# Attention, a feed-forward block and a gated convolution block in fp32 products split three ways: the places of TensorE's operands in SBUF

## The chip, the cores and the metric

The kernel runs on one core of a Trainium2 chip. Its engines are TensorE (PE: matrix products, with the load of the stationary operand shown as PEld), VectorE (DVE), ScalarE (ACT), GpSimd (POOL) and SyncE (SP, which here issues the DMAs). The metric is the time of one execution on the device in microseconds; lower is better. Three executions of the kernel before took 1298.81, 1300.61 and 1300.77 us, a median of 1300.61 us.

## The reference

The batch is 8, the sequence 576 long, the model 512 wide, so there are 4608 tokens in 36 tiles of 128.

```python
# 1. attention in chunks of 64 tokens, 8 heads of 64
scores = scale * np.matmul(q_c, k_c.transpose(0, 1, 2, 4, 3))
attn = np.exp(scores - np.max(scores, axis=-1, keepdims=True))
attn = attn / (np.sum(attn, axis=-1, keepdims=True) + 1e-09)
x = np.matmul(attn, v_c)                    # put together as [B, S, 512]
# 2. feed-forward block, 512 -> 2048 -> 512, with a residual
xn = (x - mu) / np.sqrt(var + 1e-06) * g_ln
x = x + np.maximum(xn @ w_ch1, 0.0) @ w_ch2
# 3. gated block, 512 -> 1024 -> 512
h = np.maximum(x @ w_in, 0.0)
conv_out = sum(conv_w[k] * hp[:, k:k + S] for k in range(3))   # hp: h padded by one token
out = (h * (1.0 / (1.0 + np.exp(-conv_out)))) @ w_out
```

Inputs and output are fp32.

## The kernel before

Every large product is done in the type fp32r, in which TensorE streams fp32 words. An operand is split into a high part (a cast to fp32r) and a low part (the rest), and `mm3` (lines 113 to 116) adds three products into a PSUM bank: low stationary part times high streamed part (L114), high times low (L115), high times high (L116). Each of the three is one LDWEIGHTS of a stationary operand of 128 columns and one MATMUL that streams 256 or 512 columns.

There are four such products, and they follow each other:

- **up** (w_ch1): `product` (L588) for each of 9 slabs of 512 tokens. The weights `w` (tiles `w1`) are stationary, and the normalised tokens `xc`, seven combinations of 256-column blocks per slab, are streamed: 256 columns at a time, 12 matmuls in a row on one `xc`. The 36 tiles of attention (L385 to L475, plain fp32 products of 64 columns and transposes of 128) lie between them.
- **down** (w_ch2): `Down` (L688). `split` (L700) makes `hh` and `hl`, the high and low part of a tile of the up product that was stored in HBM and loaded again as `hr`. They are stationary, the weights `w2` (trace names `w` and `wd`) are streamed, 512 columns. 12 matmuls use one `hh`/`hl`.
- **gate** (w_in): `Gate` (L884). The weights are stationary, the tokens `xb` (`x_parts`, L805: four tiles of `[128, 2, 512]` for even slabs and four for odd ones) are streamed, 512 columns.
- **out** (w_out): `outtile` (L874). 128 columns of the rings `Gh` and `Gl` (L865, one pair for each of 8 blocks of 128 features, 1152 tokens long) are stationary, the weights `wo` (trace names `w` and `wx`) are streamed, 512 columns.

The order of the work is written out by hand: a list of steps at the head (`START`), then loops in the order in which they stand (`manual_schedule`). SBUF is given out by pools, some from the left end and some from the right end, tile after tile in the order of allocation. Two tiles named `fill` of 56 floats, 224 bytes per partition, are never read or written: one ends the pool `const` (L104), the other is alone in the pool `edge` at the right end (L524, L525). With them every tile that a fp32r matmul reads starts at a multiple of 256 bytes.

**Distance** here is the byte address of the streamed operand, minus the byte address of the stationary operand that is loaded while it streams (that of the next matmul), modulo 256 bytes. The addresses are those that the built program holds. In the kernel before it is 0 for all fp32r matmuls. Of the plain fp32 work, the products of `rk` and `rq` have distance 0, those of `rv` and `pt` distance 32, the transposes of `pp` distance 64 and those of `xn` distance 128.

Of the kernel before, what the change touches and what calls it, by code (L numbers as in the profile page):

```python
# [8 lines left out]
F32 = mybir.dt.float32  # L9
F32R = mybir.dt.float32r  # L10
# [34 lines left out]
def attn_moe_moe2(  # L45
# [63 lines left out]
    def split(hi, lo, src):  # L109
        nc.scalar.copy(hi, src)  # L110
        nc.vector.tensor_tensor(out=lo, in0=src, in1=hi.bitcast(F32), op=ALU.subtract)
# [366 lines left out]
    class Slab:  # L478
# [24 lines left out]
            return {1: b11, 5: getattr(self, "t1", None), 6: b11, 2: b21, 7: b12, 4: b21, 3: b22}[n]  # L503

        def u(self, n):
            t = self.xc[n] = xc_p.tile([128, 2, 2, 256], F32R, tag=f"xc{n}", name="xc")
            nc.scalar.copy(t[:, 0], self.of(n))

        def v(self, n):
# [11 lines left out]


    with tc.manual_schedule():
        edge = tc.alloc_tile_pool(name="edge", bufs=1, side="right", reuse_waits="tile")  # L524
        edge.tile([128, 56], F32, name="fill")  # L525
        wb_p = tc.alloc_tile_pool(name="wb", bufs=1, reuse_waits="tile")
        wa_p = tc.alloc_tile_pool(name="wa", bufs=1, reuse_waits="tile")
        xc_p = tc.alloc_tile_pool(name="xc", bufs=1, side="right", reuse_waits="tile")
        su_p = tc.alloc_tile_pool(name="su", bufs=1, side="right", reuse_waits="tile")
        at = Attention()  # L530
# [15 lines left out]
        def one(step):  # L546
            kind, i = step[0], int(step[1:])
            if kind in "atmng":
                getattr(blocks[i // 4], kind)(i % 4)
            elif kind == "W":  # L550
                blocks[i // 4].W(i % 4, nc.sync)
            elif kind == "w":
                blocks[i // 4].W(i % 4, nc.scalar)
            elif kind == "s":
                blocks[i // 4].s(i % 4)
            elif kind in "hl":
                getattr(blocks[i // 7], kind)(i % 7)
            elif kind in "juv":
                getattr(slabs[0], kind)(i)
            elif kind == "S":  # L560
                at.S(i, (4, 6, 0, 4, 0, 2)[i])
            elif kind == "V":
                at.V(i, (4, 6, 0, 4)[i])
            elif kind == "P":
                at.P(i, i % 2 * 2 if i > 3 else 2)
            elif kind == "L":
                at.L(i, late=i > 5)
            elif kind in "y":
                at.x(i)
            elif kind == "z":  # L570
                at.T(i)
            else:
                getattr(at, kind)(i)
# [109 lines left out]
        for tv in range(4, NTILE, 2):  # L683

            t = 28 * (tv // 4 - 1) + (13 if tv % 4 else 0)
            session({4: 7, 6: 14}.get(tv, t), tv)

        class Down:  # L688
# [10 lines left out]

            def split(self, f):  # L700
                t = self.hr[f % 8][:, f // 8 * 2:f // 8 * 2 + 2].rearrange("p a n -> p (a n)")
                self.hh = dp.tile([128, 512], F32R, tag="hh", bufs=2, name="hh")
                self.hl = dp.tile([128, 512], F32R, tag="hl", bufs=2, name="hl")
                nc.scalar.activation(out=self.hh, in_=t, func=AF.Relu)  # L704
                nc.vector.scalar_tensor_tensor(  # L705
                    out=self.hl, in0=t, scalar=0.0, in1=self.hh.bitcast(F32), op0=ALU.max,
                    op1=ALU.subtract,
                )
                return self.hh, self.hl
# [9 lines left out]
        dp = None  # L719
        for p in range(NS + 1):  # L720
            if p + 1 < NS:
                slabs[p + 1] = Slab(p + 1)
            for G in range(4):
                for s, (n, lag) in enumerate(SLOTS):
                    t = 28 * p + 7 * G + s
# [14 lines left out]
                    if p == NS - 1:  # L740
                        if (G, s) == (0, 5):
                            at.p.release()
                            dp = tc.alloc_tile_pool(name="dp", bufs=1, reuse_waits="tile")
# [51 lines left out]
        def split_x2(i, kk):  # L795
            t = x2r[i]
            split(
                xb[i % 2][0][kk // 2][:, kk % 2].rearrange("p (a t) -> p a t", t=32),
                xb[i % 2][1][kk // 2][:, kk % 2].rearrange("p (a t) -> p a t", t=32),
                t[:, :, kk, :],  # L800
            )
            if kk == KD - 1 and i + 1 < NS:
                load_x2(i + 1)

        def x_parts(pool, name):  # L805
            return [[pool.tile([128, 2, 512], F32R, name=f"{name}{2 * i + j}") for j in range(2)]
                    for i in range(2)]

        xb = [x_parts(pbx, "xb0")]
        todo = [(p, f) for p in range(NS) for f in F_ORDER]  # L810
        downs = {0: down}
        xrs = {}
        ended = None
        for n, (p, f) in enumerate(todo):
            hh, hl = parts
# [21 lines left out]
            if (p, f) == (0, 15):  # L837
# [4 lines left out]
                for i in range(16):  # L842
                    pool, tag = wb_tags[i]
# [17 lines left out]
        pb = tc.alloc_tile_pool(name="pb", bufs=1, reuse_waits="tile")  # L861
        RING = 1152
        Gh, Gl = {}, {}

        def ring(f):  # L865
            Gh[f] = pb.tile([128, RING], F32R, name=f"Gh{f}")
            Gl[f] = pb.tile([128, RING], F32R, name=f"Gl{f}")

        for f in (7, 6, 5):
            ring(f)  # L870
        for f in range(5):
            ring(f)
        xb.append(x_parts(pb, "xb1"))
        def outtile(T, tail=False):  # L874
            ps = bank[4 + T % 4] if tail else bank[2 + T % 2]
# [114 lines left out]
        pb.release()  # L990
        pbx.release()
        wb_p.release()
        edge.release()


# [41 lines left out]
```

## Time and profile before

| what | value |
|---|---|
| median of three executions | 1300.61 us |
| profiled execution | 1302.26 us, its span 1300.5 us |
| PE busy | 1251.4 us, 96% of the span |
| PEld busy | 1097.7 us, 84% |
| DVE busy | 744.6 us, 57% |
| ACT busy | 614.7 us, 47% |
| mean granted clock of TensorE | 0.976 |

Busy time is the time in which an engine has an instruction in it. On PE matmuls overlap, and the end that a row gives to a matmul is modelled: the pace is read from starts, not from durations. Idle time of an engine that is not the bottleneck costs nothing.

### The profile page before, as it was taken

To read this page: it belongs to the slowest core of one execution; us is meant where nothing else is said; L and a number is where in the kernel's file an instruction comes from. 1 tells how busy PE (TensorE), PEld (TensorE's weight loads), DVE (VectorE), ACT (ScalarE), POOL (GpSimd) and SP (SyncE) were. 2 spreads that over 40 slices of the span, in tenths; PEclk is the share of its full clock that TensorE was granted. 3 is DMA by queue.
4 is the path that set the end of the run, shared out by engine and by line. 5 is a ranking of instruction groups with operands and counts; after the bars stand their busy time and mean duration, and the time that the engine had idled before them with its cause. 6 is when DMAs were issued, how large, how long until landed. Compare 5 with 4: busy or idle time off the path is not lost.

```text
span 1300.5 us, 23238 instructions
## 1 busy us (share of the span) xinstructions
PE 1251.4 (96%) x9096; PEld 1097.7 (84%) x9096; DVE 744.6 (57%) x1430; ACT 614.7 (47%) x1510; POOL 78.6 (6%) x172
## 2 busy tenths in 40 slices
PE   5569999999999999999999999999999999999998
PEld 4469999999999998778888888888788888888887
DVE  7896456456456457577734333433886556655550
ACT  6775555555546345344322222222675555555541
POOL 0000000000000000000000000000121111111100
PEclk6689999999999999999999999999999999999999
DMA  9724644644545268486444355432111011101001
GB/s 266 212 98 154 205 164 160 205 157 166 202 155 185 108 219 291 135 305 217 154 161 162 122 177 185 161 120 87 41 57 57 26 56 58 57 25 57 25 25 49
DMA packets 127021, 177.70 MB, mean 137 GB/s; under 512 B 12736, under 2 KB 72128, under 8 KB 126912
## 3 DMA queue, kind: packets, MB, share of 16 engines
q1 hardware_dynamic: 126912, 176.22, 40.3%
q8 instruction: 71, 1.16, 0.4%
q14 instruction: 38, 0.31, 0.1%
HBM read 110.13 MB, written 66.06 MB: 135 GB/s over the span
## 4 chain that ended last, share of the span: by engine, by line
PE 86%; DVE 5%; DMA 4%; ACT 3%; SPq 1%; issue 1%; ACTq 0%; DVEq 0%
PE banks L114 27%; PE banks L115 27%; PE banks L116 27%; PE banks L385 3%; DMA rk<-in_k_dram 2%; PE banks L467 1%; DMA w<-in_moe_w_ch_dram 1%; PE banks L425 1%; DVE w L157 1%; DMA wd<-in_moe_w_ch_dram 1%; DVE hl L705 1%; DMA x2d<-x2T 0%; DVE w L152 0%; SPq L366 0%; DVE xr L160 0%
## 5 line engine op out<-in xcount | busy, mean ns | idle before, releaser
L114 PE MATMUL banks<-xc,w 128*128 128x256 f32 x1008 | 291.7, 289 | 9.6 <-DVE u L160 6.9
L115 PE MATMUL banks<-xc,w 128*128 128x256 f32 x1008 | 287.4, 285 | 0.0
L116 PE MATMUL banks<-xc,w 128*128 128x256 f32 x1008 | 287.2, 285 | 0.0
L704 ACT ACTIVATE hh<-hr 128x512 fp32r<-128x512 f32 x144 | 91.1, 632 | 257.4 <-PE banks L116 257.0
L705 DVE SCALAR_TENSOR_TENSOR hl<-hr,hh 128x512 fp32r<-128x512 f32 x144 | 99.3, 689 | 191.5 <-ACT hh L704 189.1
L114 PEld LDWEIGHTS banks<-xc,w 128*128 128x128 f32 x1008 | 195.8, 194 | 12.1 <-DVE u L160 7.5
L115 PEld LDWEIGHTS banks<-xc,w 128*128 128x128 f32 x1008 | 196.0, 194 | 0.0
L116 PEld LDWEIGHTS banks<-xc,w 128*128 128x128 f32 x1008 | 195.6, 194 | 0.0
L114 PE MATMUL banks<-w,hl 128*128 128x512 f32 x396 | 154.8, 391 | 0.0
L115 PE MATMUL banks<-w,hh 128*128 128x512 f32 x396 | 154.1, 389 | 0.0
L116 PE MATMUL banks<-w,hh 128*128 128x512 f32 x396 | 154.1, 389 | 0.0
L160 DVE TENSOR_TENSOR u<-banks,u 128x512 f32<-128x512 f32 x108 | 74.4, 689 | 123.1 <-ACT u L614 91.5
L920 DVE SCALAR_TENSOR_TENSOR cv<-hb,cw_sb,cv 128x510 f32<-128x510 f32 (+31 forms) x256 | 117.3, 513 | 0.6
L614 ACT COPY u<-banks 128x512 f32<-128x512 f32 x108 | 63.9, 592 | 111.0 <-PE banks L116 110.3
L114 PE MATMUL banks<-xb,w 128*128 128x512 f32 x288 | 112.7, 391 | 2.2 <-ACT hb L905 1.9
L115 PE MATMUL banks<-xb,w 128*128 128x512 f32 x288 | 112.1, 389 | 0.0
L116 PE MATMUL banks<-xb,w 128*128 128x512 f32 x288 | 112.1, 389 | 0.0
L411 ACT ACTIVATE pp<-banks,mx 128x64 f32<-128x64 f32 x288 | 86.8, 335 | 26.8 <-DVE x L439 20.4
L114 PEld LDWEIGHTS banks<-w,hl 128*128 128x128 f32 x396 | 74.3, 188 | 17.6 <-DVE hl L705 2.4
L116 PEld LDWEIGHTS banks<-w,hh 128*128 128x128 f32 x396 | 74.3, 188 | 15.4
L115 PEld LDWEIGHTS banks<-w,hh 128*128 128x128 f32 x396 | 74.3, 188 | 15.3
L907 POOL COPY hal<-hb 128x2 f32<-128x2 f32 x64 | 41.8, 652 | 727.3 <-ACT hb L905 727.3
(106 smaller groups left out, 2183.1 us busy)
## 6 DMA issues: line engine op xcount, KB each, us to landing
hd<-u SPq DMA_DIRECT2D x144, 256.0 KB, 3.2
hr<-hd SPq DMA_DIRECT2D x72, 512.0 KB, 3.6
w<-in_moe_w_ch_dram SPq DMA_DIRECT2D x27, 512.0 KB, 7.2
rv<-in_v_dram SPq DMA_DIRECT2D x36, 256.0 KB, 5.5
xd<-x SPq DMA_DIRECT2D x36, 256.0 KB, 2.2
xr<-xd SPq DMA_DIRECT2D x36, 256.0 KB, 4.5
x2d<-x2T SPq DMA_DIRECT2D x36, 256.0 KB, 2.0
x2r<-x2d SPq DMA_DIRECT2D x36, 256.0 KB, 3.8
```

Source lines behind the costliest of these rows:

```text
L114: nc.tensor.matmul(ps, ll, rh, start=first, stop=False, **kw)
L115: nc.tensor.matmul(ps, lh, rl, start=False, stop=False, **kw)
L116: nc.tensor.matmul(ps, lh, rh, start=False, stop=last, **kw)
L157: nc.vector.tensor_tensor(out=out, in0=a, in1=b, op=ALU.subtract)
L160: nc.vector.tensor_tensor(out=out, in0=a, in1=b, op=ALU.add)
L385: nc.tensor.matmul(ps[half(c), e, j, :], lt[half(e), j, c, :], rt[half(e), j, c, :], start=True, stop=True,)
L411: nc.scalar.activation(out=pp[:, j, e, :], in_=self.both[T][:, e, j, :], func=AF.Exp, scale=SCALE, bias=mx[:, e, j:j + 1], accum_out=sm[:, ...
L614: nc.scalar.copy(flat(t), bank[to])
L704: nc.scalar.activation(out=self.hh, in_=t, func=AF.Relu)
L705: nc.vector.scalar_tensor_tensor(out=self.hl, in0=t, scalar=0.0, in1=self.hh.bitcast(F32), op0=ALU.max, op1=ALU.subtract,)
L907: nc.gpsimd.tensor_copy(out=hal[:, f, :], in_=hb[:, 512:514])
L920: nc.vector.scalar_tensor_tensor(out=cv[:, a:e], in0=hb[:, a + tap:e + tap], scalar=cw_sb[:, tap, f:f + 1], in1=cv[:, a:e], op0=ALU.mult, ...
```

## The change

Four kinds of tiles get room behind them or a shift inside them, and the tile at the right end of SBUF goes. An `xc` tile is 1032 floats long and its first 1024 are used; the `xb` tiles likewise; a ring is 1160 long and its first 1152 are used. Thus tiles that follow each other start 32 bytes apart modulo 256. `hh` and `hl` are 544 long, and 512 of them are used from float `f % 8 * 4` on, 16 bytes further for each `f`; their two buffers start 128 bytes apart modulo 256.

```diff
--- before.py
+++ after.py
@@ -503,7 +503,8 @@
             return {1: b11, 5: getattr(self, "t1", None), 6: b11, 2: b21, 7: b12, 4: b21, 3: b22}[n]
 
         def u(self, n):
-            t = self.xc[n] = xc_p.tile([128, 2, 2, 256], F32R, tag=f"xc{n}", name="xc")
+            t = xc_p.tile([128, 1032], F32R, tag=f"xc{n}", name="xc")[:, :1024]
+            t = self.xc[n] = t.rearrange("p (h k n) -> p h k n", h=2, k=2)
             nc.scalar.copy(t[:, 0], self.of(n))
 
         def v(self, n):
@@ -521,8 +522,6 @@
 
 
     with tc.manual_schedule():
-        edge = tc.alloc_tile_pool(name="edge", bufs=1, side="right", reuse_waits="tile")
-        edge.tile([128, 56], F32, name="fill")
         wb_p = tc.alloc_tile_pool(name="wb", bufs=1, reuse_waits="tile")
         wa_p = tc.alloc_tile_pool(name="wa", bufs=1, reuse_waits="tile")
         xc_p = tc.alloc_tile_pool(name="xc", bufs=1, side="right", reuse_waits="tile")
@@ -699,8 +698,9 @@
 
             def split(self, f):
                 t = self.hr[f % 8][:, f // 8 * 2:f // 8 * 2 + 2].rearrange("p a n -> p (a n)")
-                self.hh = dp.tile([128, 512], F32R, tag="hh", bufs=2, name="hh")
-                self.hl = dp.tile([128, 512], F32R, tag="hl", bufs=2, name="hl")
+                at = slice(f % 8 * 4, f % 8 * 4 + 512)
+                self.hh = dp.tile([128, 544], F32R, tag="hh", bufs=2, name="hh")[:, at]
+                self.hl = dp.tile([128, 544], F32R, tag="hl", bufs=2, name="hl")[:, at]
                 nc.scalar.activation(out=self.hh, in_=t, func=AF.Relu)
                 nc.vector.scalar_tensor_tensor(
                     out=self.hl, in0=t, scalar=0.0, in1=self.hh.bitcast(F32), op0=ALU.max,
@@ -803,8 +803,11 @@
                 load_x2(i + 1)
 
         def x_parts(pool, name):
-            return [[pool.tile([128, 2, 512], F32R, name=f"{name}{2 * i + j}") for j in range(2)]
-                    for i in range(2)]
+            def one(at):
+                t = pool.tile([128, 1032], F32R, name=f"{name}{at}")[:, :1024]
+                return t.rearrange("p (k n) -> p k n", k=2)
+
+            return [[one(2 * i + j) for j in range(2)] for i in range(2)]
 
         xb = [x_parts(pbx, "xb0")]
         todo = [(p, f) for p in range(NS) for f in F_ORDER]
@@ -863,8 +866,8 @@
         Gh, Gl = {}, {}
 
         def ring(f):
-            Gh[f] = pb.tile([128, RING], F32R, name=f"Gh{f}")
-            Gl[f] = pb.tile([128, RING], F32R, name=f"Gl{f}")
+            for to, name in ((Gh, "Gh"), (Gl, "Gl")):
+                to[f] = pb.tile([128, RING + 8], F32R, name=f"{name}{f}")[:, :RING]
 
         for f in (7, 6, 5):
             ring(f)
@@ -990,7 +993,6 @@
         pb.release()
         pbx.release()
         wb_p.release()
-        edge.release()
 
 
 # ---- launch: one core; inputs and outputs as the reference has them ----
```

The instructions of the built program are the same as before on every engine, in the same order and with the same waits: 6784 on PE, 1422 on DVE, 1042 on ACT, 571 on SP, 134 on POOL. Shapes and the inner steps of the operands are the same too. Addresses are what differs. The distances of the fp32r matmuls that are followed by another fp32r matmul become:

| product | matmuls | distance 0 | distances | changes from one matmul to the next |
|---|---|---|---|---|
| up | 2989 | 422 | 0, 32, ... to 192, about 430 each | 252 |
| down | 1728 | 108 | all multiples of 16, 108 each | 145 |
| gate | 864 | 128 | 0, 32, ... to 192, 79 to 224 each | 720 |
| out | 863 | 78 | 0, 32, ... to 224, 36 to 144 each | 495 |
| all | 6444 | 736 | 5708 are not 0 | 1612 |

Of the other tiles, `x2r` (the loaded tokens of the gated block), the last two `wo` tiles and the output tiles `ob` start at 224, 224 and 160 modulo 256 where before they started at 0, 0 and 32.

## Rows read from the trace of the kernel before

**Rows 1.** The page: span, busy time of the engines, PE's slices, its granted clock.

```profile
span 1300.5 us, 23238 instructions
...
PE 1251.4 (96%) x9096; PEld 1097.7 (84%) x9096; DVE 744.6 (57%) x1430; ACT 614.7 (47%) x1510; POOL 78.6 (6%) x172
...
PE   5569999999999999999999999999999999999998
...
PEclk6689999999999999999999999999999999999999
```

**Rows 2.** The chain that ended last, by engine and line.

```profile
PE 86%; DVE 5%; DMA 4%; ACT 3%; SPq 1%; issue 1%; ACTq 0%; DVEq 0%
PE banks L114 27%; PE banks L115 27%; PE banks L116 27%; PE banks L385 3%; DMA rk<-in_k_dram 2%; PE banks L467 1%; DMA w<-in_moe_w_ch_dram 1%; PE banks L425 1%; DVE w L157 1%; DMA wd<-in_moe_w_ch_dram 1%; DVE hl L705 1%; DMA x2d<-x2T 0%; DVE w L152 0%; SPq L366 0%; DVE xr L160 0%
```

**Rows 3.** Groups of instructions: out<-in, count | busy, mean ns | idle before them.

```profile
L115 PE MATMUL banks<-xc,w 128*128 128x256 f32 x1008 | 287.4, 285 | 0.0
...
L115 PE MATMUL banks<-w,hh 128*128 128x512 f32 x396 | 154.1, 389 | 0.0
...
L115 PE MATMUL banks<-xb,w 128*128 128x512 f32 x288 | 112.1, 389 | 0.0
...
L115 PE MATMUL banks<-w,Gh 128*128 128x512 f32 x216 | 84.0, 389 | 0.0
...
L115 PE MATMUL banks<-wd,hh 128*128 128x512 f32 x180 | 70.1, 389 | 0.0
...
L115 PE MATMUL banks<-wx,Gh 128*128 128x512 f32 x72 | 28.0, 389 | 0.0
...
L385 PE MATMUL banks<-rk,rq 64*64 64x64 f32 x1152 | 25.7, 237 | 14.6 <-DMA rk<-in_k_dram 13.4 <-DVE mx L402 1.0
...
L385 PE MATMUL banks<-rv,pt 64*64 64x64 f32 x1152 | 24.4, 237 | 7.1 <-ACT pt L431 7.0
```

**Rows 4.** Timeline of PE, 207.5 to 220.5: start, duration (us), instruction (first and last of 107).

```profile
207.56 0.28 PE L115 MATMUL banks<-xc,w 128*128 128x256 f32 x1
...
220.28 0.28 PE L116 MATMUL banks<-xc,w 128*128 128x256 f32 x1
```

**Rows 5.** Timeline of PE, 690 to 713: first and last of 103 rows.

```profile
689.69 0.39 PE L115 MATMUL banks<-wd,hh 128*128 128x512 f32 x1
...
712.81 0.39 PE L115 MATMUL banks<-w,hh 128*128 128x512 f32 x1
```

**Rows 6.** Timeline of all engines, 527.2 to 530.3, around a wait of PE.

```profile
528.42 0.19 PEld L114 LDWEIGHTS banks<-w,hl 128*128 128x128 f32 x1 [0.37 <-DVE hl L705]
528.42 0.50 PE L114 MATMUL banks<-w,hl 128*128 128x512 f32 x1
528.53 0.19 PEld L115 LDWEIGHTS banks<-w,hh 128*128 128x128 f32 x1
...
528.76 0.40 PE L115 MATMUL banks<-w,hh 128*128 128x512 f32 x1
...
529.91 0.39 PE L114 MATMUL banks<-w,hl 128*128 128x512 f32 x1
```

**Rows 7.** Timeline of PE, 525.3 to 527.3, after another wait.

```profile
525.42 0.50 PE L114 MATMUL banks<-w,hl 128*128 128x512 f32 x1
525.76 0.40 PE L115 MATMUL banks<-w,hh 128*128 128x512 f32 x1
...
527.16 0.40 PE L115 MATMUL banks<-w,hh 128*128 128x512 f32 x1
```

**Rows 8.** Timeline of PE, 205.5 to 208.6: two transposes of attention.

```profile
205.70 1.04 PE L425 MATMUL banks<-ident,pp 128*128 128x128 f32 x8
206.57 1.04 PE L467 MATMUL banks<-ident,xn 128*128 128x128 f32 x8
```

**Rows 9.** DMA issues: out<-in, count, KB each, median us to landing.

```profile
x2r<-x2d SPq DMA_DIRECT2D x36, 256.0 KB, 3.8
```

## The prediction

> **What bounds the kernel now.** I read the page first. PE is busy for 1251.4 of 1300.5 us, from the fourth of its 40 slices on nearly without a hole, and from the same slice on the granted clock is at nine tenths or more; DVE and ACT have an instruction in them for 57% and 47% of the span [rows 1]. The chain of waits says the same: 86% of it is PE, and three lines, L114 to L116, have 27% each [rows 2]. These are the three products of `mm3`. So the end is set by the pace of the fp32r matmuls, and the next thing to know is that pace and how much of it is not streaming.
>
> The groups by line give the counts [rows 3]: each of the three lines has 1008 matmuls of 256 columns and 396 + 288 + 216 + 180 + 72 = 1152 of 512 columns, so there are 3024 short and 3456 long ones. The pace is read from starts in the timeline, since ends are modelled. Short: 106 steps from 207.56 to 220.28 us, 120.0 ns each [rows 4]. Long: 102 steps from 689.69 to 712.81 us, 226.7 ns each [rows 5]. 3024 x 120.0 + 3456 x 226.7 is 1146 us, 88% of the span: the whole kernel is these two numbers, and attention is most of the rest.
>
> The two paces differ by 106.7 ns for 256 columns, 0.417 ns a column, which is the 2.4 GHz level. Streaming alone is then 106.7 and 213.3 ns, and both paces are 13.3 ns above it. That remainder is the same for a short and a long matmul, so it does not go with the streamed columns; it goes with the change of matmul or with the load of 128 stationary columns, which is there once in each.
>
> **What the change touches.** No instruction is removed, added or moved on any engine, and no wait differs. So the sum has one term: 5708 matmuls that stream while the next stationary operand is read, at a distance other than 0, times the change of pace that this brings. 736 keep distance 0. The term has no cover: PE does not wait for another engine in these stretches, so every nanosecond of pace is a nanosecond of the end.
>
> Two smaller edits I cost at nothing. ACT and DVE write and read the shifted tiles at other starts; both are idle for about half of the span [rows 1], and a slower PE gives them more time. The transfers into `x2r` land at another place modulo 256; they take 3.8 us [rows 9], four to a slab, and a slab of the gated block is worked on for some 8 x 12 x 226.7 ns = 22 us in the gate product alone; only the first slab's are awaited. If each of those took an eighth longer, the loss there is about half a microsecond.
>
> **Price of the term.** The trace of before has no fp32r matmul at another distance, so the price must come from the nearest rows, with a bound on each side.
>
> What shows that the two reads of PE can get in each other's way at all are the rows after a wait. At 528.42 PE starts again after 0.37 us without a stationary operand [rows 6]. Its first matmul is modelled at 0.50 us, the next load starts 0.11 us late, and the next matmul starts 340 ns later. From there on the load is issued with the matmul again, as always, but the pace isn't yet the steady one: 5 steps from 528.76 to 529.91 us are 230.0 ns each [rows 6], and 6 steps from 525.76 to 527.16 us after another wait are 233.3 ns each [rows 7]. Together 11 steps take 2.55 us, 231.8 ns each, 5.1 ns above the steady 226.7, and the matmuls at the start of this are 0.40 us long and not 0.39. Same instructions, same tiles, same clock: what differs is how the streamed read and the stationary read lie to each other in time. After some matmuls PE falls into the steady pace again and keeps it for the rest of the stage. I read this as two reads that collide until they have found an order in which they do not. A distance modulo 256 shifts the same two reads against each other in place instead of in time, so I take 5.1 ns as the price of a distance other than 0.
>
> Bound above: the load is not hidden at all. After a wait, the step from the first matmul to the second is 340 ns [rows 6, 7], 113 ns above the steady pace. At all 5708 matmuls that would be 645 us. It is far from the value I take, since there the load was issued late and here it is not; but if one distance in eight had it, it would be 713 x 113 = 81 us. Bound below: the whole remainder of 13.3 ns is a collision that distance 0 itself causes, and it goes: 5708 x 13.3 = -76 us.
>
> 5708 x 5.1 = +29.1 us. Against the profiled execution, 1302.3 us, that is 1331.4 us; this execution lay 1.65 us above the median of the three that were timed, so the forecast is **1330 us**, 2.2% more than 1300.6. The short matmuls may get less than this: they have the same load of 128 columns but a shorter stream to absorb it in, so they may also get more; with none for the 2567 of them the sum is 3141 x 5.1 = 16 us, with twice the price 42 us.
>
> One rule of the Trainium skill speaks against this. "TensorE: Matmul & The Clock Gate", in "Step-by-step: what each phase is for", says that PE has two independent read ports to SBUF, one for the streamed operand and one for LDWEIGHTS, and that loading the next weights takes no read bandwidth from the running matmul. By that rule the distance can't matter and the time stays at 1300.6 us. The rows after a wait speak against it, as far as they go: the same pair of reads ran 5.1 ns slower for 11 steps. They don't refute it, since a pipeline that fills again could look the same.
>
> **Rivals.**
>
> No effect: 1300.6 us, 1297 to 1303. For it: at plain fp32 the distance shows nothing. The products of `rk` and `rq` at distance 0 and those of `rv` and `pt` at distance 32 both have a mean of 237 ns over 1152 matmuls [rows 3], and 8 transposes at distance 64 take 0.87 us from 205.70 to 206.57, 108.8 ns each [rows 8], right behind the fp32r ones, without a sign of trouble. Against it: those stream at most 128 columns, and a 128-column transpose takes 108.8 ns, about as long as 256 columns of fp32r, so its words come at half the rate; two reads that collide at the full rate could well miss each other there.
>
> Faster, on the other side: distance 0 is the place where both reads want the same part of SBUF at every step, and the 13.3 ns are its price. At other distances the pace falls toward the streaming time. If it all went, 1302.3 - 76 - 1.7 = 1225 us; if half, 1263 us. For it: the remainder of the transposes at distance 64 is small, if their 128 columns are taken as 256 steps of the array: 108.8 against 106.7 ns, so 2 ns and not 13. And 13.3 ns is 32 steps at 2.4 GHz, one for each four words of the 128 that a load reads in a partition, a number that a collision at each would give. Against it: the remainder is the same to 0.1 ns over a hundred steps of either kind [rows 4, 5], which looks like a fixed cost of an fp32r matmul, and pairs of reads that collide should show the unsteady paces that rows 6 and 7 do show. It decides from the point where more than half of the distances have a pace below 226 and 120 ns.
> The same page of the Trainium skill, "TensorE: Matmul & The Clock Gate", in "Back-to-back issue gap", says that a warm step is the streaming time plus 2.5 ns, 109.2 and 215.8 ns here; the steady paces are 10.8 ns above it, so an estimate by that rule, if distance 0 were the reason, is 5708 x 10.8 = -62 us, or about 1239 us.
>
> Slower by resettling: not the distance itself costs, but each change of it, since PE must find its order again. There are 1612 changes. In up and down the distance stays for 12 matmuls, and 397 changes at 6 steps of 5.1 ns are 12 us; in gate and out it changes at nearly every matmul, 1215 x 5.1 = 6 us. Together 18 us, 1319 us. It lies inside the forecast's range and differs in its shape: in a run of 12 matmuls with one distance the last would be at 120 or 227 ns again.
>
> Much slower: some distances make every word of the load collide, so that the load is not hidden there. One in eight of them gives the 81 us above, 1382 us. The after trace would have two or more separate paces, one of them far above the other, by distance.
>
> **How the numbers follow.** Slower by collisions, in one of its three forms, has 0.58: the only rows that show the two reads in another relation are slower ones. No effect has 0.24, for the plain fp32 rows. Faster has 0.18, for the unexplained 13.3 ns. The measurement of this kernel can tell about 0.2% (2.6 us) from no change, so these three are also the chances of slower, same and faster. The likeliest case's own range is 1310 to 1400 us. The range of 8 in 10 goes from 1292 to 1405 us: below it lies most of the faster case (about 0.14), above it the far end of the slower one (about 0.06).
>
> **What will show it right or wrong.** The order on all engines is the same, so the steps can be compared one by one. If I am right, starts within one `xc` lie more than 120 ns apart and within one `hh` more than 227 ns, by an amount that depends on the distance; the matmuls at distance 0 (one `xc` in seven, one `hh` in sixteen) keep 120.0 and 226.7 ns; PE's share stays at 96% or rises; waits of ACT and DVE for PE get longer. The forecast is wrong in kind if all distances have the paces of before (no effect), or paces below them (faster), or if the time goes anywhere else than into the step from one matmul to the next: into waits of PE for `hl`, `xc` or a transfer. It is wrong in size alone if the step depends on the distance but by another price than 5.1 ns.

## The result and the profile after

Four executions of the changed kernel took 1309.80 to 1311.77 us, with a median of 1310.53; four of the kernel before on the same chip had a median of 1299.86. The ratio is 1.0083, 95% interval 1.0066 to 1.0101: slower by 0.8%. 1330 us was forecast, within 1292 to 1405. The direction and the place were right; the size was about a third of what I gave.

The page of the profiled execution (1309.8 us) shows the span, the busy times, PE's slices and its granted clock.

```profile
span 1308.0 us, 23238 instructions
...
PE 1262.1 (96%) x9096; PEld 1093.6 (84%) x9096; DVE 744.2 (57%) x1430; ACT 614.7 (47%) x1510; POOL 76.7 (6%) x172
...
PE   5569999999999999999999999999999999999998
...
PEclk6689999999999999999999999999999999999999
```

PE is the bound as before and its clock is the same slice for slice [rows 1], so what it gained or lost is in the steps. The groups by line (count | busy, mean ns of one) answer to those of before.

```profile
L115 PE MATMUL banks<-xc,w 128*128 128x256 f32 x1008 | 285.2, 283 | 0.0
...
L115 PE MATMUL banks<-w,hh 128*128 128x512 f32 x396 | 156.0, 394 | 0.0
...
L115 PE MATMUL banks<-xb,w 128*128 128x512 f32 x288 | 113.1, 393 | 0.0
...
L115 PE MATMUL banks<-w,Gh 128*128 128x512 f32 x216 | 85.0, 393 | 0.0
...
L115 PE MATMUL banks<-wd,hh 128*128 128x512 f32 x180 | 70.5, 392 | 0.0
...
L115 PE MATMUL banks<-wx,Gh 128*128 128x512 f32 x72 | 28.5, 396 | 0.0
...
L385 PE MATMUL banks<-rk,rq 64*64 64x64 f32 x1152 | 25.8, 237 | 12.6 <-DMA rk<-in_k_dram 12.4
```

A modelled duration follows the step here. The mean of a long matmul went from 389 ns to 392 to 396 in all of down, gate and out; that of a short one went the other way, from 285 to 283; `rk` and `rq`, whose tiles weren't shifted against each other, stayed at 237 [rows 3].

Since both programs have the same instructions in the same order, the starts can be subtracted one by one. From matmul to matmul the changed kernel is longer by 6.8 us in down, 3.7 in gate and 4.1 in out, shorter by 5.0 in up and by 2.0 in attention and its waits: 7.6 us, the difference of the two spans before rounding. Attention differs by -1.4 us in down160 and by +1.4 us in xc_sweep below, where tiles of other products alone are moved, so its 2.0 us can't be put down to the change. (The timed medians lie 10.7 us apart. This profiled execution is the fastest of its four, that of before was above its median.)

Sorted by distance the steps separate. These are rows of the timeline of PE of the changed kernel: the first and the last of twelve matmuls of down at distance 160, the same at distance 0, and three of the twelve of up at distance 192.

```profile
711.81 0.40 PE L116 MATMUL banks<-w,hh 128*128 128x512 f32 x1
...
714.39 0.39 PE L115 MATMUL banks<-w,hh 128*128 128x512 f32 x1
```

```profile
722.94 0.39 PE L116 MATMUL banks<-w,hh 128*128 128x512 f32 x1
...
725.43 0.39 PE L115 MATMUL banks<-wd,hh 128*128 128x512 f32 x1
```

```profile
447.85 0.28 PE L114 MATMUL banks<-xc,w 128*128 128x256 f32 x1
...
448.21 0.28 PE L114 MATMUL banks<-xc,w 128*128 128x256 f32 x1
...
449.11 0.28 PE L116 MATMUL banks<-xc,w 128*128 128x256 f32 x1
```

At 160, 11 steps take 2.58 us, 234.5 ns each. At 0, in the same stage, 11 steps take 2.49 us, 226.4 ns, the pace of before [rows 5]. At 192 in up the first three steps take 0.36 us, 120 ns each, and the next eight 0.90 us, 113 ns each: a pace that the kernel before never has in a settled stretch [rows 4].

### The profile page after: what moved, and what is told of

The parts are those of the page before. It is cut to its first block, busy times and chain, and to the rows that moved or that the text cites. A ratio compares the mean times of both kernels' runs of the same rounds, so it can differ in the third digit from the quotient of the medians.

```text
span 1308.0 us, 23238 instructions
## 1 busy us (share of the span) xinstructions
PE 1262.1 (96%) x9096; PEld 1093.6 (84%) x9096; DVE 744.2 (57%) x1430; ACT 614.7 (47%) x1510; POOL 76.7 (6%) x172
## 4 chain that ended last, share of the span: by engine, by line
PE 86%; DVE 6%; DMA 3%; ACT 3%; SPq 1%; issue 1%; ACTq 0%; DVEq 0%
PE banks L114 27%; PE banks L116 27%; PE banks L115 27%; PE banks L385 3%; PE banks L467 1%; DMA rk<-in_k_dram 1%; DVE w L157 1%; PE banks L425 1%; DVE hl L705 1%; DMA wd<-in_moe_w_ch_dram 1%; DMA w<-in_moe_w_ch_dram 0%; DMA x2d<-x2T 0%; DVE w L152 0%; DVE u L160 0%; DVE cy L146 0%
## 5 line engine op out<-in xcount | busy, mean ns | idle before, releaser
L114 PE MATMUL banks<-xc,w 128*128 128x256 f32 x1008 | 289.8, 287 | 9.1 <-DVE u L160 7.0
L116 PE MATMUL banks<-xc,w 128*128 128x256 f32 x1008 | 285.2, 283 | 0.0
L115 PE MATMUL banks<-xc,w 128*128 128x256 f32 x1008 | 285.2, 283 | 0.0
L114 PEld LDWEIGHTS banks<-xc,w 128*128 128x128 f32 x1008 | 192.9, 191 | 11.7 <-DVE u L160 7.6
L115 PEld LDWEIGHTS banks<-xc,w 128*128 128x128 f32 x1008 | 192.7, 191 | 0.0
L116 PEld LDWEIGHTS banks<-xc,w 128*128 128x128 f32 x1008 | 192.7, 191 | 0.0
L114 PE MATMUL banks<-w,hl 128*128 128x512 f32 x396 | 156.6, 395 | 0.0
L116 PE MATMUL banks<-w,hh 128*128 128x512 f32 x396 | 156.2, 394 | 0.0
L115 PE MATMUL banks<-w,hh 128*128 128x512 f32 x396 | 156.0, 394 | 0.0
L160 DVE TENSOR_TENSOR u<-banks,u 128x512 f32<-128x512 f32 x108 | 74.3, 689 | 120.6 <-ACT u L613 89.5
L923 DVE SCALAR_TENSOR_TENSOR cv<-hb,cw_sb,cv 128x510 f32<-128x510 f32 (+31 forms) x256 | 117.2, 512 | 0.6
L114 PE MATMUL banks<-xb,w 128*128 128x512 f32 x288 | 113.9, 395 | 1.8 <-ACT hb L908 1.5
L116 PE MATMUL banks<-xb,w 128*128 128x512 f32 x288 | 113.9, 396 | 0.0
L115 PE MATMUL banks<-xb,w 128*128 128x512 f32 x288 | 113.1, 393 | 0.0
L114 PEld LDWEIGHTS banks<-w,hl 128*128 128x128 f32 x396 | 74.4, 188 | 19.5 <-DVE hl L705 2.3
L115 PEld LDWEIGHTS banks<-w,hh 128*128 128x128 f32 x396 | 74.5, 188 | 17.4
L116 PEld LDWEIGHTS banks<-w,hh 128*128 128x128 f32 x396 | 74.4, 188 | 17.3
```

The costliest lines, as they stand in the source:

```text
L114: nc.tensor.matmul(ps, ll, rh, start=first, stop=False, **kw)
L115: nc.tensor.matmul(ps, lh, rl, start=False, stop=False, **kw)
L116: nc.tensor.matmul(ps, lh, rh, start=False, stop=last, **kw)
L160: nc.vector.tensor_tensor(out=out, in0=a, in1=b, op=ALU.add)
L923: nc.vector.scalar_tensor_tensor(out=cv[:, a:e], in0=hb[:, a + tap:e + tap], scalar=cw_sb[:, tap, f:f + 1], in1=cv[:, a:e], op0=ALU.mult, ...
```

## The experiments

All change the kernel before, by the same means as the change. A kernel for which no ratio is given was executed once. "Before" for each is the runs of the kernel before on the same chip (1300.2 to 1300.9 us). Steps by distance are worked out from all starts in a run's trace.

**Is it the distance, or the place of an operand?** Both fill tiles are resized, so that all operands of the fp32r matmuls move by 64 bytes together.

```diff
-    const.tile([128, 56], F32, name="fill")
+    const.tile([128, 72], F32, name="fill")
-        edge.tile([128, 56], F32, name="fill")
+        edge.tile([128, 40], F32, name="fill")
```

> Everything that a fp32r matmul reads is moved by 64 bytes together, so all distances stay 0 but no operand starts at a multiple of 256 bytes. If the distance sets the pace: steps stay 120.0 and 226.7 ns, time within 2 us of before (1300 us). If the place of an operand by itself costs (a start that is no multiple of 256 bytes): the paces that distance 64 showed in the changed kernel, about 230 ns long and 118.3 ns short, 3456 x 3.5 - 3024 x 1.7 ns = +7 us, 1307 us.

Measured: 1301.9 us, ratio 1.0011 (1.0002 to 1.0020). The groups by line:

```profile
L115 PE MATMUL banks<-xc,w 128*128 128x256 f32 x1008 | 287.6, 285 | 0.0
...
L115 PE MATMUL banks<-w,hh 128*128 128x512 f32 x396 | 154.1, 389 | 0.0
```

Both means are those of before to the nanosecond, and by starts the four products differ from before by 0.3 us or less each. So the place alone costs nothing in the steps, and the 1307 us expected of it are far outside the interval; that falls. (The median is 1.6 us above before, and the interval leaves out 1.0000. The profile shows none of this in the products, and its cause stays open.) What counts is how the two operands lie to each other.

**Do the parts add up?** Three kernels, each with one part of the change; where the tile `edge` goes, a fill tile elsewhere keeps the rest at distance 0.

```diff
# down_only: hh and hl as in the change, nothing else
+                at = slice(f % 8 * 4, f % 8 * 4 + 512)
+                self.hh = dp.tile([128, 544], F32R, tag="hh", bufs=2, name="hh")[:, at]
+                self.hl = dp.tile([128, 544], F32R, tag="hl", bufs=2, name="hl")[:, at]
# up_only: xc as in the change, edge goes, pbx ends with a fill tile
+            t = xc_p.tile([128, 1032], F32R, tag=f"xc{n}", name="xc")[:, :1024]
+        pbx.tile([128, 56], F32, name="fill")
# gate_out: xb and the rings as in the change, edge goes, xc_p ends with a fill tile
+                t = pool.tile([128, 1032], F32R, name=f"{name}{at}")[:, :1024]
+                to[f] = pb.tile([128, RING + 8], F32R, name=f"{name}{f}")[:, :RING]
+        xc_p.tile([128, 56], F32, name="fill")
```

> Only hh and hl are shifted. If the distance sets the pace matmul by matmul: down as in the changed kernel, mean step about 231.5 ns against 227.9, +6.8 us, 1306.6 us; up, gate and out at 120.0 and 226.7 ns. If the loss comes from something that the stages share (waits, transfers): less than 3 us here.

> Only the xc tiles are apart. If the distance sets the pace and short matmuls gain by it: up as in the changed kernel, about -5 us, 1295 us. If a distance other than 0 always costs, as I forecast, and the gain in up of the changed kernel was chance: +5 us or more.

> Only the xb tiles and the rings are apart, with the same distances in gate and out as in the changed kernel. If the distance sets the pace: gate +3.7 us and out +4.1 us, 1307.7 us, and the three parts add up to the change (+6.8 - 5.0 + 7.8 = +9.6 us). If the distance matters only while it stays for some matmuls: gate and out, where it changes at nearly every matmul, stay within 2 us of before.

Measured: 1307.11 us (ratio 1.0049, 1.0034 to 1.0064), 1295.00 us (0.9959, 0.9945 to 0.9973) and 1307.72 us (1.0055, 1.0040 to 1.0070), against 1300.34. The groups by line of each, in this order:

```profile
L115 PE MATMUL banks<-xc,w 128*128 128x256 f32 x1008 | 287.3, 285 | 0.0
...
L115 PE MATMUL banks<-w,hh 128*128 128x512 f32 x396 | 156.0, 394 | 0.0
...
L115 PE MATMUL banks<-xb,w 128*128 128x512 f32 x288 | 112.1, 389 | 0.0
```

```profile
L115 PE MATMUL banks<-xc,w 128*128 128x256 f32 x1008 | 284.9, 283 | 0.0
...
L115 PE MATMUL banks<-w,hh 128*128 128x512 f32 x396 | 154.1, 389 | 0.0
```

```profile
L115 PE MATMUL banks<-w,hh 128*128 128x512 f32 x396 | 154.1, 389 | 0.0
...
L115 PE MATMUL banks<-xb,w 128*128 128x512 f32 x288 | 113.1, 393 | 0.0
...
L115 PE MATMUL banks<-w,Gh 128*128 128x512 f32 x216 | 85.0, 393 | 0.0
```

In each kernel the group whose distances changed has the mean of the changed kernel, and the others have that of before. The three differences are +6.8, -5.3 and +7.4 us, together +8.8 against the 10.7 of the whole change, within what the intervals leave. So the loss is in the steps of each product by itself, nothing that the stages share, and up gained.

**Is 192 good for all of up?** A fill tile of 64 bytes at the end of `xc_p` puts all seven `xc` tiles at distance 192 and leaves everything else at 0.

```diff
+        xc_p.tile([128, 16], F32, name="fill")
         xc_p.release()
```

> All xc tiles at distance 192, everything else at distance 0 as before. In the changed kernel the last nine of twelve steps at distance 192 were 113.7 ns. If the short matmuls settle at that pace for as long as the distance stays: 3024 x 6.3 ns = -19 us, about 1281 us, faster than both kernels. If the pace there came from the neighbouring distances or from a pause at a change of xc: short steps near 118 ns, 1294 us or more.

Measured: 1287.77 us against 1300.17, ratio 0.9903 (0.9886 to 0.9919). This beats both kernels, by one unread tile. It is less than the 19 us expected: by starts, up is 13.2 us shorter. The page, and two stretches of the timeline of PE, the first and last row of 100 and of 49:

```profile
span 1286.1 us, 23238 instructions
...
PE 1237.6 (96%) x9096; PEld 1083.1 (84%) x9096; DVE 743.7 (58%) x1430; ACT 614.0 (48%) x1510; POOL 78.0 (6%) x172
```

```profile
475.11 0.28 PE L116 MATMUL banks<-xc,w 128*128 128x256 f32 x1
...
486.33 0.28 PE L116 MATMUL banks<-xc,w 128*128 128x256 f32 x1
```

```profile
184.23 0.28 PE L115 MATMUL banks<-xc,w 128*128 128x256 f32 x1
...
189.89 0.28 PE L115 MATMUL banks<-xc,w 128*128 128x256 f32 x1
```

The first stretch has 99 steps of 113.3 ns, the second 48 of 117.9, with the same tiles and the same distance. 2146 of the steps in up are at 113 or 114 ns and 695 between 116 and 119; either pace lasts for dozens of matmuls and goes over into the other at an interruption (a few products or transposes of attention between them). Of 39 stretches of nine steps or more without an interruption, from 100 us on, read from their fourth step, 32 are at the first pace throughout and 7 at the second. The granted clock is 1.00 at both paces, and the load of the DMA engines doesn't separate them: its share is 0.93 in a slow stretch (455 to 463 us) and 0.49 in one of fast products (214 to 226 us). So a distance does not fix the pace alone: at 192 there are two that hold. Which one follows is settled at an interruption; how, is not shown.

**Which distances?** Seven at a time on the `xc` tiles, each tile with its own padding and shift (the numbers are those of xc_sweep, xc_words has others):

```diff
+    XC_AT = {4: (0, 0), 6: (8, 4), 7: (0, 0), 5: (8, 4), 3: (8, 4), 2: (8, 4), 1: (32, 4)}
-            t = self.xc[n] = xc_p.tile([128, 2, 2, 256], F32R, tag=f"xc{n}", name="xc")
+            pad, at = XC_AT[n]
+            t = xc_p.tile([128, 1024 + pad], F32R, tag=f"xc{n}", name="xc")[:, at:at + 1024]
+            t = self.xc[n] = t.rearrange("p (h k n) -> p h k n", h=2, k=2)
```

> The seven xc tiles at distances 112, 144, 176, 192, 208, 224 and 240, the rest as before: steps by distance between those that were looked at so far. If distances near 0 keep the settled pace of distance 0, as 16 and 240 do for long matmuls: 240 at 120.0 ns. If 192 lies in a group of good ones: 176 or 208 near 113.7 ns too; if it stands alone: those at 117 ns or more. Up as a whole -3 to -12 us.

> The seven xc tiles at distances 200, 188, 148, 100, 80, 48 and 16, some of them no multiples of 16, the rest as before. If the pace of 113.7 ns belongs to the surroundings of 192: 188 and 200 below 116 ns. If it belongs to single distances, as the single words of hh showed for long matmuls: 188 and 200 at 117 to 120 ns. If 100 suits short matmuls as it suits long ones (226.9 ns): one steady pace there. Up as a whole -3 to -10 us.

And for down, shifts of `hh` and `hl` by single words:

```diff
-                at = slice(f % 8 * 4, f % 8 * 4 + 512)
+                at = slice(f % 8 * 1, f % 8 * 1 + 512)
```

(the minus line is that of down_only).

> hh and hl shifted by single words (4 bytes) and not by four: distances 0, 252, 248 ... 228 and 128, 124 ... 100. If only the distance in place counts: the steps go over smoothly from 226.7 ns (0 to about 240) to about 232 ns, whether or not the shift is a multiple of 16 bytes. If the reads come in units of 16 bytes: all words within one unit have one pace, 252 to 240 at 226.7 ns as at 240, 236 to 228 higher. If a start that is no multiple of 16 bytes costs a unit more: odd words slower by some ns than both neighbours that are multiples of 16.

Measured: 1296.91, 1297.66 and 1306.80 us, one execution each; up -6.4 and -3.4 us in the first two, down +6.4 us in the last. Mean step in ns from the fourth of each twelve on, without those that contain a wait or an interruption; the first value of a distance with two is from the changed kernel.

| distance | short (up) | long (down) | distance | short (up) | long (down) |
|---|---|---|---|---|---|
| 0 | 119.5 | 226.7, 226.8 | 148 | 121.2 | not tried |
| 16 | 115.2 | 226.7 | 160 | 117.5 | 234.2 |
| 32 | 117.6 | 233.4 | 176 | 119.2 | 232.3 |
| 48 | 118.4 | 231.9 | 188 | 119.4 | not tried |
| 64 | 117.6 | 229.0 | 192 | 113.7, 114.3 | 233.5 |
| 80 | 120.0 | 229.7 | 200 | 120.0 | not tried |
| 96 | 119.0 | 233.3 | 208 | 118.7 | 233.3 |
| 100 | 120.6 | 226.7 | 224 | 118.0 | 233.4 |
| 104 | not tried | 231.1 | 228 | not tried | 235.0 |
| 108 | not tried | 233.3 | 232 | not tried | 231.1 |
| 112 | 116.6 | 228.9, 227.4 | 236 | not tried | 233.3 |
| 116 | not tried | 233.6 | 240 | 117.2 | 226.7, 227.4 |
| 120 | not tried | 232.8 | 244 | not tried | 229.8 |
| 124 | not tried | 229.2 | 248 | not tried | 230.8 |
| 128 | 119.0 | 232.1, 232.3 | 252 | not tried | 232.4 |
| 144 | 118.2 | 232.9 |  |  |  |

No long step is shorter on the mean than at distance 0; 16, 100 and 240 equal it. 252 and 248, nearer to 0 than 240, are 4 to 6 ns slower, and 100 lies among slow ones (96 and 104). For short steps 192 has the lowest mean, with 188 and 200 at 119 to 120, 176 and 208 at 119, and 240 not at the 120.0 of distance 0. So neither "smooth in the distance" nor "in units of 16 bytes" holds: the good distances are single ones, and of the three readings of hh_words none came out. Multiples of 16 have no favour as such (100 is none), and 100 does not suit short ones (120.6).

These means mix paces, since a distance stays for twelve matmuls only. Two stretches of down in the changed kernel, both at distance 112, and one of up at distance 16, in xc_words (timeline of PE, first and last row of 9, of 11 and of 9):

```profile
598.26 0.40 PE L116 MATMUL banks<-wd,hh 128*128 128x512 f32 x1
...
600.13 0.40 PE L115 MATMUL banks<-wd,hh 128*128 128x512 f32 x1
```

```profile
686.80 0.39 PE L116 MATMUL banks<-wd,hh 128*128 128x512 f32 x1
...
689.07 0.39 PE L114 MATMUL banks<-wd,hl 128*128 128x512 f32 x1
```

```profile
206.75 0.28 PE L114 MATMUL banks<-xc,w 128*128 128x256 f32 x1
...
207.66 0.28 PE L116 MATMUL banks<-xc,w 128*128 128x256 f32 x1
```

By unrounded starts the mean steps are 233, 227 and 113 ns. Distance 112 holds either long pace, and 16 reaches the short pace of 192. Over the last six steps of each twelve, long ones are at 226.7 ns in all nine at 0, 16 and 100, in five to eight of nine at 112, in seven of nine at 124, in eight or nine of nine at 240, and never lower (the changed kernel, down_only and hh_words). Short ones are at 113 ns at 192 in most twelves, at 16 in 15 of 36, at 112 in 14 of 36, and at 64 and 144 in one each. So 192 does not stand alone, and 16 and 112 have the best pace seen for either kind; whether they would hold it through a whole product was not tried.

**Does the change of distance cost, or the distance?** A fill tile of 96 bytes ahead of `hh` puts down at distance 160 throughout; in a second kernel the same tile stands between `hh` and `hl`, so that `hl` alone is at 160.

```diff
# down160
+                            dp.tile([128, 24], F32, name="fill")
                             parts = down.split(0)
# hl160: ahead of the first hl
+                if not gap:
+                    gap.append(dp.tile([128, 24], F32, name="fill"))
```

> All hh and hl at distance 160, for the whole of down without a change. If the distance sets the pace: 234 ns as at 160 in the changed kernel, 1728 x 7.6 ns = +13 us, about 1313 us. If only the changes of distance cost and PE settles afterwards: 226.7 ns after the first dozen, time as before.

> Only hl is moved, to distance 160; hh stays at 0. Of the three matmuls of a group, L114 has hl loaded already and hh being loaded, L115 has hh loaded and hh being loaded, L116 has hh loaded and the next hl being loaded. If the operand that is loaded during the stream counts: steps of L116 are the long ones (about 234 ns), L114 and L115 near 226.7 ns. If the operand that is loaded already counts: L114 is the long one. If PE carries the effect from one step to the next, as gate and out at distance 0 showed (232 ns): all three are above 226.7 ns. Down +4 to +11 us.

Measured: 1311.67 us (down +10.8 us) and 1310.23 us (down +8.2 us). The first was expected at +13 us: the steps are as long as that asks for, but PE's waits in down are 1.7 us shorter, so a little of the pace is covered. The timeline of PE of the first, eight matmuls in a row:

```profile
689.41 0.40 PE L116 MATMUL banks<-wd,hh 128*128 128x512 f32 x1
689.65 0.40 PE L114 MATMUL banks<-wd,hl 128*128 128x512 f32 x1
689.88 0.39 PE L115 MATMUL banks<-wd,hh 128*128 128x512 f32 x1
690.12 0.40 PE L116 MATMUL banks<-wd,hh 128*128 128x512 f32 x1
690.35 0.40 PE L114 MATMUL banks<-wd,hl 128*128 128x512 f32 x1
690.58 0.39 PE L115 MATMUL banks<-wd,hh 128*128 128x512 f32 x1
690.82 0.39 PE L116 MATMUL banks<-wd,hh 128*128 128x512 f32 x1
691.05 0.40 PE L114 MATMUL banks<-wd,hl 128*128 128x512 f32 x1
```

By unrounded starts the seven steps are 238, 237, 231, 234, 235, 234 and 231 ns, and they repeat in that order for as long as I followed them (25 steps from 689.4 us on), with a mean of 234.3. Nothing changes from one matmul to the next but the time, and PE doesn't settle at 226.7. So a constant distance costs, and the pace is a pattern over several matmuls.

The groups by line of the second kernel, L114 to L116 of down:

```profile
L114 PE MATMUL banks<-w,hl 128*128 128x512 f32 x396 | 157.0, 396 | 0.0
L115 PE MATMUL banks<-w,hh 128*128 128x512 f32 x396 | 156.8, 396 | 0.0
L116 PE MATMUL banks<-w,hh 128*128 128x512 f32 x396 | 156.0, 394 | 0.0
```

By starts the steps are 232.7, 233.2 and 231.7 ns. All three are slow, also L115, which at distance 0 streams against and beside the same operand `hh`. So this run can't say which of the two stationary operands, the loaded one or the one being loaded, counts; it shows that a slow neighbour makes a step slow that would be fast in a row of its own. Gate and out of the changed kernel say the same: their steps at distance 0 have a mean of 231.9 and 232.1 ns, since the distance there changes at most matmuls.

## Why the prediction was right and wrong

- *The bound, and where the time would go.* Right. The clock is unchanged, PE is at 96%, and the time is in the steps from one fp32r matmul to the next. "No cover" holds nearly: PE's waits in down are 0.6 us shorter in the changed kernel.
- *The price of a long step, 5.1 ns from the rows after a wait.* Right on the mean, and partly by luck: 3141 long steps at 5.1 ns were 16.0 us; down, gate and out have 14.6 us more, 4.6 ns a step. But this is a mean of prices by distance that go in down from 0 (16, 240) to 7.5 ns (160), and other distances would have given another. That the rows after a wait and those at another distance have one cause, the loss of a settled order, was argued and not shown.
- *"5708 x 5.1 = +29.1 us".* This is the step that failed. The rows after a wait were all of long matmuls [rows 6, 7], and I charged the same to the 2567 short ones, 13 us. Up, where they are, gained 5.0 us, and up_only, which moves their tiles alone, is 5.3 us shorter than before. I had named the case with no price for them (16 us, or 1317 us) as a side remark and looked for no row on it, though the trace of before has it: after a wait of PE at 487.2 us the short matmuls do this (timeline of the kernel before):

```profile
487.70 0.39 PE L114 MATMUL banks<-xc,w 128*128 128x256 f32 x1 [0.26 <-DVE u L160]
...
487.92 0.28 PE L115 MATMUL banks<-xc,w 128*128 128x256 f32 x1
...
488.51 0.28 PE L114 MATMUL banks<-xc,w 128*128 128x256 f32 x1
...
488.99 0.28 PE L115 MATMUL banks<-xc,w 128*128 128x256 f32 x1
```

From 487.92 to 488.51 us five steps take 0.59 us, 118 ns each (119, 118, 125, 113 and 119 by unrounded starts), before they settle at 120: here the settled pace is not the fastest. Behind 26 of the 27 interruptions by attention from 130 to 450 us there are one or two steps of 117 to 119 ns in the same way, and then 120. Charged with the 1.2 to 2 ns that this is below 120, the short ones give -3 to -5 us, and the sum would have been 1300.6 + 16.0 less this, 1312 to 1314 us.
- *Faster, "distance 0 is the place where both reads want the same part".* Not for long matmuls at any distance tried. For short ones half of it is true: at 192, and for some twelves at 16 and 112, the 13.3 ns above streaming become 6.7 (113.3 - 106.7). The prediction had the two kinds move together.
- *The rule of two ports ("TensorE: Matmul & The Clock Gate", "Step-by-step: what each phase is for", in the Trainium skill).* The trace disagrees with the conclusion that I drew from it: the distance between the streamed and the stationary operand alone moves the mean long step by up to 8 ns (226.7 to 235.0), with no instruction changed. The 2.5 ns that "Back-to-back issue gap" on that page of the Trainium skill gives, as the gap of an isolated matmul and not of a stream of load and matmul pairs as here, was reached at no distance; the least that holds here is 6.7 ns.
- *Slower by resettling.* Partly: at 16 and 240 the long steps come back to 226.7 within three steps, and in gate and out the changes make even distance 0 slow. But down160 has no change of distance and is the slowest kernel, 1311.67 us, so it isn't the whole.
- *Much slower.* No step pattern came near the 340 ns of a load that is not hidden; the worst settled mean is 235.0 ns (distance 228, in hh_words).
- *"The matmuls at distance 0 keep 120.0 and 226.7 ns."* Right in down, right in up after some steps, wrong in gate and out.

What stays open is the cause inside TensorE. That the streamed read and the load collide in SBUF was argued only: no run took the load away, and none tells which stationary operand matters. Why single distances are good, and what leads PE into one of two paces at the same distance, no run shows either.

## What to carry to other kernels

Where PE's rows stand back to back and each matmul has its own load, read the step from the starts, for each number of streamed columns apart, and look at the steps after a wait of each kind: if they differ from the settled step, the relation of the operands' addresses is worth a trial. Keep that relation constant over a stage, try the few values for one product at a time with a tile that nobody reads, and take the best one for each product: of those held through a whole product here (0 and 192 for up, 0 and 160 for down) that is 0 for 512 columns and 192 for 256, which made it 1.0% faster than the kernel before (ratio 0.9903, 0.9886 to 0.9919). A mean over a few matmuls at one distance can mix two paces; read the steps one by one before a value is dropped. A price read from one shape is not a price for another.

## What the runs showed that I had not expected

- One distance can have two steps that both hold, 113.3 and 117.9 ns at 192 for short matmuls, 227 and 233 ns at 112 for long ones; at 192 the step changed over only at interruptions.
- At a fixed distance the steps of like matmuls need not be equal: 160 has a cycle of seven, 231 to 238 ns.
- Single words matter: 252 against 0 is 232.4 against 226.7 ns, and 100 against 104 is 226.7 against 231.1.
